# A linear-attention and PReLU feed-forward kernel: q of batch 0 loaded whole and first, w_out read in runs of four rows, w_in's columns taken with a step of four

## The chip, the cores and the metric

The kernel runs on one core of one Trainium2 chip. The metric is the time of one execution on the device in microseconds (us). The kernel before has a median of 294.09 us over 13 runs, which lie between 293.6 and 296.61 us.

## What is computed

The inputs are float32: q, k and v of shape (8, 8, 576, 64), g_norm (64), w_in (512, 2048), w_out (2048, 512) and alpha (2048). The output is (4608, 512) in float32.

```
kv  = einsum('bhsd,bhse->bhde', k, v)
o   = einsum('bhsd,bhde->bhse', q, kv)
o   = o / sqrt(mean(o*o, -1) + 1e-6) * g_norm
x   = o.transpose(0, 2, 1, 3).reshape(4608, 512)
h   = x @ w_in
g   = max(h, 0) + alpha * min(h, 0)
out = g @ w_out
```

The order of the 2048 columns of h is free: any permutation that is applied to the columns of w_in, to alpha and to the rows of w_out alike leaves the output as it is. The change uses this.

## The kernel before

**Tiling.** There are nine windows (`w`) of 512 tokens and 16 groups (`g`) of 128 columns of the hidden width. For a window, `m1_mm` makes one group of h with four matmuls of 128x512 (line 478), `m1_evac` turns it into fp16 `gt` with one ScalarE and one VectorE instruction (lines 485 and 487), and `y_mm` multiplies by a block of w_out (line 505). In window w the groups of h of that window alternate with four `y_mm` matmuls of window w-1.

**Attention.** k and q come into staging tiles `kst` and `qst` with 64 columns of a head beside each other, and `regroup` (line 112) copies them into `ksb` and `qsb`, where a pair of heads is one run of 128. `step_kv` (line 245) makes the k-v products of pairs of heads, `step_ot` and `half_ot` multiply by q, `ssq_mm` and `half_ssq` sum the squares and take the reciprocal root on ScalarE (Ln, then Exp), and `norm` writes `xt`, the input of the first product. Batches 0 and 1 transpose q on TensorE (`step_t`, line 221). From batch 2 on, q is transposed by DMA (line 383), and tiles go through four steps `tile_a` to `tile_d`: the product, the sum of squares on VectorE (line 409), the factor `rg` on GpSimd (line 421), and the product `xrow` on VectorE (line 430), which a DMA transpose (line 435) puts into `xm`.

**Order.** The order on every engine is written out by hand, and engines run their instructions in that order. `keep_warm(n)` issues n matmuls of 128x512 that nobody reads, to fill waits of TensorE at the start. `phase_steps(w + 1)` spreads the attention work of window w+1 over the groups of window w: `lags` says how many groups lie between `tile_a`, `tile_b` and `tile_c` (second entry), and `tile_d` (third entry). During window 1, `ys` are four PSUM banks with partial sums of window 0, and h uses the pools `H_POOL[0]`, `H_POOL[2]`, `S_POOL`, `H_POOL[1]` in turn.

**Loads.** All loads of q, k, v and of the weights are issued by GpSimd and turn float32 into fp16. Their order is: for each half of the heads of batch 0 its q, k and v (12 DMAs, since each piece is split into a long part, line 97, and a short part, line 102), then the four blocks of w_in, k of batch 1, the first block of w_out, q and v of batch 1, the other three blocks of w_out (line 173), then q, k and v of batch 2. Eight semaphores serve these DMAs in turn, so a DMA is issued once the eighth before it has landed.

A block of w_in has 512 neighbouring columns, and group r of it takes 128 neighbouring ones. A block of w_out has 512 rows, and partition p holds rows p, 128 + p, 256 + p and 384 + p, each a run of 2,048 bytes.

Of the kernel before, what the change touches and what calls it, by code (L numbers as in the profile page):

```python
# [17 lines left out]
def kernel(  # L18
# [27 lines left out]
    NC = D_MODEL // P  # L46
    assert NC == NPAIR and 0 < REM < P
    inv_d = 1.0 / D
    NB_PE = 2

    const_p = ctx.enter_context(tc.tile_pool(name="constp", bufs=1))
# [59 lines left out]
    def regroup(b, nm, h0=0, h1=H, eng=None):  # L111
        (eng or nc.vector).tensor_copy(  # L112
            out=bufs[b % NBUF][nm][:, :, h0:h1, :].rearrange("p t h d -> p h t d"),
            in_=stages[b % NBUF][nm][:, h0:h1],
        )
# [12 lines left out]
    ident = const_p.tile([P, P], FP32, name="ident")  # L128
    make_identity(nc, ident[:])
    HH = H // 2  # L130
    for h0 in (0, HH):
        for nm in "qkv":
            load(0, nm, h0, h0 + HH)

    mask32 = const_p.tile([P, P], FP32, name="mask32")
# [14 lines left out]
    g2col = const_p.tile([P, 1], FP32, name="g2col")  # L150
    nc.sync.dma_start(out=g2col[0:64, :], in_=g_norm[:].unsqueeze(1))
    nc.sync.dma_start(out=g2col[64:128, :], in_=g_norm[:].unsqueeze(1))
    alpha_row = const_p.tile([NF, P], FP32, name="alpha_row")
    nc.sync.dma_start(out=alpha_row[:], in_=moe_alpha[:].rearrange("(g p) -> g p", p=P))


    WQ = 4
    w_in_sb = []
    w_out_sb = []
    FW = D_FF // WQ  # L160
    GW = NF // WQ

    def load_w_in(i):
        t = w_p.tile([P, NC, FW], FP16, name=f"w_in_sb{i}")
# [6 lines left out]
    def load_w_out(i):  # L171
        t = w_p.tile([P, GW, D_MODEL], FP16, name=f"w_out_sb{i}")
        nc.gpsimd.dma_start(
            out=t[:],
            in_=moe_w_out[i * GW * P : (i + 1) * GW * P, :].rearrange("(g p) m -> p g m", p=P),
        )
        w_out_sb.append(t)

    def w_in_blk(c, g):
        i, r = divmod(g, GW)  # L180
        return w_in_sb[i][:, c, r * P : (r + 1) * P]

    def w_out_blk(g):
        i, r = divmod(g, GW)
# [50 lines left out]
    def step_kv(b, j0=0, j1=NPAIR, pool=(ps_s, "s")):  # L235
        if j0 == 0:
            kv_sb = attn_p.tile([P, NPAIR, P], FP16, name="kv_sb")
            for j in range(NPAIR):
                kvs[b, j] = kv_sb[:, j, :]
            kvs[b] = kv_sb  # L240
        kv_ps = pool[0].tile([P, j1 - j0, P], FP32, name="kv_ps", tag=pool[1])
        for j in range(j0, j1):
            ks, vs = pair_cols(b, "k", j), pair_cols(b, "v", j)
            for t in range(NT):
                nc.tensor.matmul(  # L245
                    out=kv_ps[:, j - j0, :], lhsT=ks(t), rhs=vs(t),
                    start=(t == 0), stop=(t == NT - 1),
                )
        nc.vector.tensor_mul(
            out=kvs[b][:, j0:j1, :], in0=kv_ps[:],  # L250
            in1=mask32[:].unsqueeze(1).to_broadcast([P, j1 - j0, P]),
        )
# [136 lines left out]
    def next_o():  # L389
        n_tile[0] += 1  # L390
        return ps_o, f"o{(n_tile[0] - 1) % 3}"
# [48 lines left out]
    def phase_steps(w):  # L440


        if w >= NW:
            return []
        todo = [(b, t) for b in range(NB_PE, min(B, w + 1)) for t in range(NT)
                if (b, t) not in done and b * S + t * P < (w + 1) * W]
        done.update(todo)
        steps = []

        kv_at = {NB_PE: 3, NB_PE + 1: 6, NB_PE + 2: 2}.get(w, 0)  # L450
        n = {NB_PE: 4, NB_PE + 1: 2}.get(w, 0)
        steps += [([], [], []) for i in range(n)]

        lags = (0, 1, 4) if w == NB_PE else (0, 1, 2)
        if w in (NB_PE + 1, NB_PE + 2):
            k = [b for b, t in todo].index(w)
            todo[k:k] = [None] * (3 if w == NB_PE + 1 else 1)
        for i in range(len(todo) + lags[2]):
            a, b, d = (
                [todo[i - k]] if 0 <= i - k < len(todo) and todo[i - k] else [] for k in lags  # L460
            )
            begin = [lambda x=x: tile_b(*x) for x in b] + [lambda x=x: tile_d(*x) for x in d]
            mid = [lambda x=x: tile_c(*x) for x in b]
            end = [lambda x=x: tile_a(*x) for x in a]
            steps.append((begin, mid, end))
        if w < B:
            steps[kv_at][1].append(lambda: step_kv(w, pool=next_o() if kv_at else (ps_s, "s")))
        return steps

    done = set()  # L470
# [10 lines left out]
            )  # L481

    def m1_evac(h_ps, w, g):
        m_sb = gt_p.tile([P, W], FP32, name="m_sb", bufs=3)
        nc.scalar.activation(out=m_sb[:], in_=h_ps[:], func=AF.Relu, scale=-1.0)  # L485
        gt = gt_p.tile([P, W], FP16, name="gt", tag=f"gt{g}")
        nc.vector.scalar_tensor_tensor(  # L487
            out=gt[:], in0=m_sb[:], scalar=beta_sb[:, g : g + 1], in1=h_ps[:],
            op0=ALU.mult, op1=ALU.add,
        )  # L490
        gts[w, g] = gt
# [38 lines left out]
    def spread_g():  # L530
# [13 lines left out]
    )  # L544
    step_t(0, 0, H_POOL[0])
    step_t(0, 1, H_POOL[1], nc.scalar)
    regroup(0, "k", 0, HH)
    load_rest()
    keep_warm(8)
    step_kv(0, 0, 2)  # L550
    keep_warm(2)
    step_ot(0, 0)
    step_ot(0, 1)
    keep_warm(1)
    regroup(0, "q", HH, H)
    ssq_mm(0, 0)
    step_t(0, 2, H_POOL[2])
    step_t(0, 3, H_POOL[0])
    alpha_ps = ps_h.tile([P, NF], FP32, name="alpha_ps", tag="h1")
    nc.tensor.matmul(  # L560
        out=alpha_ps[:], lhsT=alpha_row[:], rhs=ident[0:NF, 0:NF], is_transpose=True,
        start=True, stop=True,
    )

    beta_sb = const_p.tile([P, NF], FP32, name="beta_sb")
    nc.vector.tensor_scalar(
        out=beta_sb[:], in0=alpha_ps[:], scalar1=-1.0, scalar2=1.0, op0=ALU.mult, op1=ALU.add,
    )
    ssq_mm(0, 1)
    regroup(0, "k", HH, H)  # L570
    spread_g()
    norm(0, 0)
    keep_warm(2)
    step_kv(0, 2, 4)
    keep_warm(2)
    load_batch(2)
    half_ot(0, (ps_s, "s"))
    norm(0, 1)
    half_ot(1, (ps_y, "y"), nc.vector)
    first = [ps_h.tile([P, W], FP32, name="h_ps", tag=f"h{g}") for g in range(3)]  # L580
    first += [ps_o.tile([P, W], FP32, name="h_ps", tag=f"o{g}") for g in range(2)]
    half_ssq(0, O2)
    for g in range(4):
        m1_mm(first[g], 0, g, (0,))
    for g in range(4):
        if g == 2:
            half_ssq(1, O2)
        m1_mm(first[g], 0, g, (1,))
    for i in range(2):
        for c in (2, 3):  # L590
            for g in range(4):
                m1_mm(first[g], 0, g, (c,), slice(i * HW, (i + 1) * HW))
                if (i, c) == (1, 3):
                    m1_evac(first[g], 0, g)
        if i == 0:
            m1_mm(first[4], 0, 4, (0, 1))
# [66 lines left out]
    for w in range(1, NW):  # L663
        steps = phase_steps(w + 1)
        for g in range(NF):
            if g == LOAD_G and 4 < w + 2 < B:
                load_batch(w + 2)
            a, part = divmod(g, TPW)
            parts = range(part * TPW, (part + 1) * TPW)
            if w == 1:  # L670
                a, y = TPW - 1, ys[TPW - 1]
                parts = [LATER + g] if LATER + g < NF else []
            begin, mid, end = steps.pop(0) if steps else ([], [], [])
            for f in begin:
                f()
            m1_group(w, g, [H_POOL[0], H_POOL[2], S_POOL, H_POOL[1]][g % 4] if w == 1 else None)
            for f in mid:
                f()
            if 0 in parts:
                pool, tag = ((ps_y, "y"), (ps_s, "s"))[a % 2]  # L680
                y = pool.tile([P, W], FP32, name="y_ps", tag=tag)
            for gg in parts:
                y_mm(y, w - 1, a, gg)
            if NF - 1 in parts:
                y_out(y, w - 1, a)
            for f in end:
                f()
            if (w, g) == (1, 0):
                regroup(2, "k", eng=nc.gpsimd)
            if (w, g) == (1, 2):  # L690


                gate = const_p.tile([1, 1], FP16, name="gate")
                nc.gpsimd.tensor_copy(out=gate[:], in_=qtms[2][0:1, 0, 0:1])
                load(3, "q")
                load(3, "k")
            if (w, g) == (1, 8):
                regroup(3, "q", eng=nc.gpsimd)
            if (w, g) == (1, 11):

                nc.gpsimd.tensor_copy(out=gate[:], in_=xm(2)[0:1, 0, W - 1 : W])
                load(3, "v")
                transpose_q(3)
                regroup(3, "k", eng=nc.gpsimd)
            for i in {5: (0, 1), 6: (2, 3), 7: (4,), 8: (5,)}.get(g, ()) if w == 2 else ():
                load_part(4, "qkv"[i // 2], i % 2 == 0)
            if w > 1 and g == LOAD_G + 3 + 3 * (w == 2) and w + 2 < B:
                regroup_batch(w + 2)
            if w > 1 and g == NF - 3 and w + 2 < B:
                transpose_q(w + 2)  # L710
# [43 lines left out]
```

## Time and profile before

| What | Value |
|---|---|
| Median of 13 runs | 294.09 us |
| The profiled execution, its own time | 294.84 us |
| Its span in the profile | 292.7 us |
| Granted TensorE clock | 0.998 |
| TensorE busy | 281.5 us (96% of the span) |
| Weight loads busy | 138.2 us (47%) |
| VectorE, ScalarE, GpSimd busy | 169.2, 152.8, 100.1 us |
| Bytes read from HBM | 36.71 MB |

The span is the time from the first to the last instruction of the program; the execution's own time is 2.14 us longer. Busy shares are averages over the whole span, so they do not say which engine a stage waits for. For that one reads the idle time ahead of an instruction and what ended it, and the chain of work that ended last.

### The profile page before, as it was taken

What the parts mean: (1) busy time and instruction counts of PE and PEld (TensorE: products, weight loads), DVE (VectorE), ACT (ScalarE), POOL (GpSimd) and SP (SyncE); (2) the same over time, 40 slices, a digit from 0 to 9 for tenths busy, and PEclk for the clock granted to TensorE, in tenths of its full rate; (3) what the DMA queues carried; (4) which work ended last, traced back from release to release, by engine and by line L of the source; (5) the groups of instructions that cost most, each with busy time, mean ns of one, the idle gap of its engine ahead of it and who ended that gap; (6) DMA issues with size and microseconds to landing.
All of it is one profiled execution on the core that took longest, in us unless ns stands there. A gap on an engine that the chain in (4) does not pass through costs nothing.

```text
span 292.7 us, 4287 instructions
## 1 busy us (share of the span) xinstructions
PE 281.5 (96%) x1551; PEld 138.2 (47%) x1551; DVE 169.2 (58%) x261; ACT 152.8 (52%) x297; POOL 100.1 (34%) x111
## 2 busy tenths in 40 slices
PE   5999889999999999999999999999999999999994
PEld 2554444543454454455445544554445444444443
DVE  4579846787668476447844874488447644444300
ACT  1459357585646466447644754466448544444211
POOL 8832420584448227333743383324003200000000
PEclk9999999999999999999999999999999999999999
DMA  6999999999999925991599269925212311122133
GB/s 82 186 206 203 200 207 196 186 184 176 137 146 190 180 35 84 199 213 36 93 196 219 52 106 181 199 55 83 54 36 56 81 36 38 45 47 48 43 72 72
DMA packets 66228, 35.54 MB, mean 121 GB/s; under 512 B 32784, under 2 KB 61728, under 8 KB 66208
## 3 DMA queue, kind: packets, MB, share of 16 engines
q0 software_dynamic: 29664, 18.35, 45.6%
q1 hardware_dynamic: 36384, 16.80, 29.0%
q8 instruction: 12, 0.20, 0.3%
q10 hardware_dynamic: 160, 0.13, 0.2%
q14 instruction: 8, 0.07, 0.1%
HBM read 36.71 MB, written 9.44 MB: 158 GB/s over the span
## 4 chain that ended last, share of the span: by engine, by line
PE 76%; DMA 17%; DVE 2%; POOL 2%; ACT 1%; issue 1%; POOLq 0%; DVEq 0%
PE y_ps L505 38%; PE h_ps L478 33%; DMA vst<-in_v_dram 5%; DMA w_in_sb<-in_moe_w_in_dram 5%; DMA w_out_sb<-in_moe_w_out_dram 5%; PE kv_ps L245 2%; PE otm_ps L397 2%; DMA kst<-in_k_dram 2%; DVE gt L487 1%; DMA xm<-xrow 1%; POOL w_in_sb L165 1%; DVE ss L409 1%; DVE xrow L430 1%; ACT sqm_sb L403 0%; POOL qst L97 0%
## 5 line engine op out<-in xcount | busy, mean ns | idle before, releaser
L487 DVE SCALAR_TENSOR_TENSOR gt<-m_sb,beta_sb,h_ps 128x512 f16<-128x512 f32 x144 | 105.7, 744 | 75.4 <-ACT m_sb L485 74.9
L485 ACT ACTIVATE m_sb<-h_ps 128x512 f32<-128x512 f32 x144 | 85.5, 597 | 87.6 <-PE h_ps L478 86.3
L505 PE MATMUL y_ps<-w_out_sb,gt 128*128 128x512 f16 (+1 forms) x528 | 128.8, 373 | 0.0
L478 PE MATMUL h_ps<-xm,w_in_sb 128*128 128x512 f16 x448 | 115.0, 379 | 0.7 <-DMA xm<-xrow 0.7
L505 PEld LDWEIGHTS <-gt 128*128 128x128 f16 x592 | 57.6, 98 | 64.5
L478 PEld LDWEIGHTS <-w_in_sb 128*128 128x128 f16 x584 | 55.8, 98 | 62.2 <-issue 2.4
L421 POOL TENSOR_TENSOR rg<-ss,g_all 128x512 f32<-128x512 f32 (+1 forms) x30 | 31.3, 1042 | 78.1 <-ACT ss L419 69.8
L478 PE MATMUL h_ps<-xt,w_in_sb 128*128 128x512 f16 (+1 forms) x136 | 30.4, 366 | 0.2 <-ACT y_sb L515 0.2
L515 ACT COPY y_sb<-y_ps 128x512 f32<-128x512 f32 (+1 forms) x32 | 18.4, 575 | 15.9 <-PE y_ps L505 15.9
L409 DVE TENSOR_REDUCE ss<-sqm_sb 128x8 f32<-128x512 f32 (+1 forms) x30 | 20.5, 683 | 10.5 <-ACT sqm_sb L403 10.5
L430 DVE TENSOR_TENSOR xrow<-otm_ps,rg 128x512 f16<-128x512 f32 (+1 forms) x30 | 20.5, 682 | 3.6 <-POOL rg L421 3.6
L403 ACT ACTIVATE sqm_sb<-otm_ps 128x512 f32<-128x512 f32 (+1 forms) x30 | 17.7, 590 | 6.3 <-PE otm_ps L397 6.3
L112 POOL COPY ksb<-kst 128x2560 f16<-128x2560 f16 x6 | 13.9, 2324 | 14.8 <-DMA kst<-in_k_dram 14.8
L112 POOL COPY qsb<-qst 128x2560 f16<-128x2560 f16 x5 | 11.6, 2317 | 10.8 <-issue 10.8
L397 PEld LDWEIGHTS <-qtm 128*128 128x128 f16 x120 | 9.2, 98 | 7.1
L204 PE MATMUL warm_ps<-warm,mask 128*128 128x512 f16 x25 | 8.5, 478 | 3.3 <-DVE eps_t L146 3.3
L397 PE MATMUL otm_ps<-kv_sb,qtm 128*128 128x128 f16 x120 | 11.6, 219 | 0.0
L245 PE MATMUL kv_ps<-vst,ksb 128*128 128x128 f16 x160 | 10.4, 219 | 0.9 <-DMA vst<-in_v_dram 0.7
L245 PEld LDWEIGHTS <-ksb 128*128 128x128 f16 x160 | 9.4, 98 | 3.8 <-issue 1.7
L416 ACT ACTIVATE ss<-ss,eps_t 128x8 f32<-128x8 f32 (+1 forms) x30 | 9.0, 301 | 3.2 <-DVE ss L409 2.9
L513 DVE COPY y_sb<-y_ps 128x256 f32<-128x256 f32 x1 | 0.4, 423 | 13.4 <-PE y_ps L505 13.4
L102 POOL DMA_DIRECT2D vst<-in_v_dram x9 | 6.3, 697 | 4.3 <-DMA w_in_sb<-in_moe_w_in_dram 2.0
(76 smaller groups left out, 136.1 us busy)
## 6 DMA issues: line engine op xcount, KB each, us to landing
out_dram<-y_sb SPq DMA_DIRECT2D x70, 128.0 KB, 2.3
kst<-in_k_dram POOLq DMA_DIRECT2D x7, 320.0 KB, 8.4
qst<-in_q_dram POOLq DMA_DIRECT2D x7, 320.0 KB, 5.1
vst<-in_v_dram POOLq DMA_DIRECT2D x7, 320.0 KB, 10.7
w_in_sb<-in_moe_w_in_dram POOLq DMA_DIRECT2D x4, 512.0 KB, 10.2
w_out_sb<-in_moe_w_out_dram POOLq DMA_DIRECT2D x4, 512.0 KB, 15.2
kst<-in_k_dram POOLq DMA_DIRECT2D x7, 256.0 KB, 9.4
qst<-in_q_dram POOLq DMA_DIRECT2D x7, 256.0 KB, 6.7
```

The source lines that it names most:

```text
L112: (eng or nc.vector).tensor_copy(out=bufs[b % NBUF][nm][:, :, h0:h1, :].rearrange("p t h d -> p h t d"), in_=stages[b % NBUF][nm][:, h0:h1],)
L245: nc.tensor.matmul(out=kv_ps[:, j - j0, :], lhsT=ks(t), rhs=vs(t), start=(t == 0), stop=(t == NT - 1),)
L397: nc.tensor.matmul(out=ot_ps[:, 2 * j : 2 * j + 2, :], lhsT=qtms[b][:, t * NPAIR + j, :], rhs=kvs[b, j], start=True, stop=True,)
L403: nc.scalar.activation(out=sq[0:n], in_=ot_ps[0:n], func=AF.Square)
L409: nc.vector.tensor_reduce(out=ss[0:n], in_=sq[0:n], op=ALU.add, axis=mybir.AxisListType.X,)
L421: nc.gpsimd.tensor_tensor(out=rg[0:n], in0=ss[0:n].unsqueeze(2).to_broadcast([n, H, D]), in1=g_all[0:n].unsqueeze(1).to_broadcast([n, H, D ...
L430: nc.vector.tensor_mul(out=x[0:n], in0=ot_ps[0:n], in1=rg[0:n])
L478: nc.tensor.matmul(out=h_ps[:, cols], lhsT=w_in_blk(c, g), rhs=xt_of(w, c)[:, cols], start=(c == 0), stop=(c == NC - 1 and cols.stop == W),)
L485: nc.scalar.activation(out=m_sb[:], in_=h_ps[:], func=AF.Relu, scale=-1.0)
L487: nc.vector.scalar_tensor_tensor(out=gt[:], in0=m_sb[:], scalar=beta_sb[:, g : g + 1], in1=h_ps[:], op0=ALU.mult, op1=ALU.add,)
L505: nc.tensor.matmul(out=y[:], lhsT=gts[w, g][:, a * P : (a + 1) * P], rhs=w_out_blk(g)[:, cols], start=(g == 0), stop=(g == NF - 1),)
L515: nc.scalar.copy(out=y_sb[:, cols], in_=y[:])
```

## The change

- **q of batch 0** is loaded with all eight heads in two DMAs ahead of everything else, in place of two DMAs for each half. k and v of batch 0 are still loaded in halves, behind it. Batch 0 takes 10 DMAs in place of 12.
- **w_out** is read with partition p holding rows 4p to 4p+3 of a block, which are one run of 8,192 bytes. Column r of such a four stands in group r, so `w_in_blk` takes every fourth column of its block: 128 fp16 elements with a step of 8 bytes. alpha is read as 4 rows of 512, transposed with four small matmuls in place of one, and `m1_evac` looks its column up as `u`.
- **The order at the start**: all four transposes of q, the transposes of alpha and `spread_g` now stand ahead of the first `step_kv`. The second `step_t` copies of a pair, the squares of `step_ot(0, 1)` and those of `half_ot(1)` change engines; `half_ssq(0)` and `half_ot(1)` move between the first matmuls of h, and `half_ssq(1)` behind the second four. The sum of the `keep_warm` matmuls stays 25.
- **Window 1**: the third lag for window 2 goes from 4 to 3, `step_kv` of batch 2 moves behind the `y_mm` of its group, and the h pools of groups 1 and 2 (of every four) change places.

```diff
     HH = H // 2
+    load(0, "q")
     for h0 in (0, HH):
-        for nm in "qkv":
+        for nm in "kv":
             load(0, nm, h0, h0 + HH)
...
-    alpha_row = const_p.tile([NF, P], FP32, name="alpha_row")
-    nc.sync.dma_start(out=alpha_row[:], in_=moe_alpha[:].rearrange("(g p) -> g p", p=P))
+    alpha_row = const_p.tile([WQ, FW], FP32, name="alpha_row")
+    nc.sync.dma_start(out=alpha_row[:], in_=moe_alpha[:].rearrange("(i f) -> i f", f=FW))
...
-            in_=moe_w_out[i * GW * P : (i + 1) * GW * P, :].rearrange("(g p) m -> p g m", p=P),
+            in_=moe_w_out[i * GW * P : (i + 1) * GW * P, :].rearrange("(p r) m -> p r m", p=P),
...
-        return w_in_sb[i][:, c, r * P : (r + 1) * P]
+        return w_in_sb[i][:, c, r:FW:GW]
...
-        lags = (0, 1, 4) if w == NB_PE else (0, 1, 2)
+        lags = (0, 1, 3) if w == NB_PE else (0, 1, 2)
...
-            steps[kv_at][1].append(lambda: step_kv(w, pool=next_o() if kv_at else (ps_s, "s")))
+            steps[kv_at][2 if w == NB_PE else 1].append(lambda: step_kv(w, pool=next_o() if kv_at else (ps_s, "s")))
...
+        u = g % GW * WQ + g // GW
...
-            out=gt[:], in0=m_sb[:], scalar=beta_sb[:, g : g + 1], in1=h_ps[:],
+            out=gt[:], in0=m_sb[:], scalar=beta_sb[:, u : u + 1], in1=h_ps[:],
...
     step_t(0, 1, H_POOL[1], nc.scalar)
-    regroup(0, "k", 0, HH)
-    load_rest()
-    keep_warm(8)
-    step_kv(0, 0, 2)
-    keep_warm(2)
-    step_ot(0, 0)
-    step_ot(0, 1)
-    keep_warm(1)
     regroup(0, "q", HH, H)
-    ssq_mm(0, 0)
     step_t(0, 2, H_POOL[2])
-    step_t(0, 3, H_POOL[0])
+    step_t(0, 3, H_POOL[0], nc.scalar)
     alpha_ps = ps_h.tile([P, NF], FP32, name="alpha_ps", tag="h1")
-    nc.tensor.matmul(
-        out=alpha_ps[:], lhsT=alpha_row[:], rhs=ident[0:NF, 0:NF], is_transpose=True,
-        start=True, stop=True,
-    )
+    for r in range(GW):
+        nc.tensor.matmul(
+            out=alpha_ps[:, r * WQ : (r + 1) * WQ], lhsT=alpha_row[:, r:FW:GW],
+            rhs=ident[0:WQ, 0:WQ], is_transpose=True, start=True, stop=True,
+        )
...
+    spread_g()
+    regroup(0, "k", 0, HH)
+    load_rest()
+    keep_warm(7)
+    step_kv(0, 0, 2)
+    keep_warm(2)
+    step_ot(0, 0)
+    step_ot(0, 1, eng=nc.vector)
+    regroup(0, "k", HH, H)
+    keep_warm(2)
+    ssq_mm(0, 0)
+    keep_warm(2)
     ssq_mm(0, 1)
-    regroup(0, "k", HH, H)
-    spread_g()
+    step_kv(0, 2, 4)
     norm(0, 0)
-    keep_warm(2)
-    step_kv(0, 2, 4)
     keep_warm(2)
     load_batch(2)
     half_ot(0, (ps_s, "s"))
     norm(0, 1)
-    half_ot(1, (ps_y, "y"), nc.vector)
...
-    half_ssq(0, O2)
     for g in range(4):
         m1_mm(first[g], 0, g, (0,))
+        if g == 1:
+            half_ssq(0, O2)
+            half_ot(1, (ps_y, "y"))
     for g in range(4):
-        if g == 2:
-            half_ssq(1, O2)
         m1_mm(first[g], 0, g, (1,))
+    half_ssq(1, O2)
...
-            m1_group(w, g, [H_POOL[0], H_POOL[2], S_POOL, H_POOL[1]][g % 4] if w == 1 else None)
+            m1_group(w, g, [H_POOL[0], S_POOL, H_POOL[2], H_POOL[1]][g % 4] if w == 1 else None)
```

More of the change, by code (lines that the diff above doesn't have):

```diff
@@ L48 @@
     inv_d = 1.0 / D
+    WQ = 4
+    FW = D_FF // WQ
+    GW = NF // WQ
     NB_PE = 2
@@ L152 @@
     nc.sync.dma_start(out=g2col[64:128, :], in_=g_norm[:].unsqueeze(1))
-    alpha_row = const_p.tile([NF, P], FP32, name="alpha_row")
-    nc.sync.dma_start(out=alpha_row[:], in_=moe_alpha[:].rearrange("(g p) -> g p", p=P))
-    WQ = 4
+    alpha_row = const_p.tile([WQ, FW], FP32, name="alpha_row")
+    nc.sync.dma_start(out=alpha_row[:], in_=moe_alpha[:].rearrange("(i f) -> i f", f=FW))
     w_in_sb = []
     w_out_sb = []
-    FW = D_FF // WQ
-    GW = NF // WQ
     def load_w_in(i):
```

## The prediction

> **What bounds the kernel now.** I read the page's slices first, then the chain of waits in order of time, then TensorE's timeline around each wait, then the busy time by stage. The page:
>
> ```profile
> PE   5999889999999999999999999999999999999994
> DMA  6999999999999925991599269925212311122133
> ```
>
> TensorE is full but for the ends, and the DMA engines are full for the first 14 slices of 7.3 us. The chain of waits, in order of time (start, us, what):
>
> ```profile
> 3.43 5.47 DMA kst<-in_k_dram
> ...
> 12.22 13.97 DMA w_in_sb<-in_moe_w_in_dram
> 26.48 13.73 DMA w_out_sb<-in_moe_w_out_dram
> 40.49 14.04 DMA vst<-in_v_dram
> 54.66 1.28 PE kv_ps L245 x20
> ...
> 66.86 2.62 DMA xm<-xrow
> 69.62 1.02 PE h_ps L478 x4
> ```
>
> Up to 54.5 us the end is set by loads, up to 69.6 us by the chain from batch 2 to xm, and then by matmuls alone. Busy time by stage (stretch, its length, busy us and instructions of PE, PEld, DVE, ACT, POOL; clock; DMA share; GB/s):
>
> ```profile
> 38.00:42.60 4.60, 4.27 (x38) 2.47 (x36) 2.08 (x3) 2.07 (x4) 1.35 (x2) 1.00 1.24 207
> 45.00:51.00 6.00, 6.00 (x31) 2.71 (x30) 4.05 (x7) 4.55 (x8) 0.00 (x0) 1.00 1.40 198
> 72.00:102.00 30.00, 30.00 (x173) 14.97 (x172) 18.63 (x28) 17.10 (x36) 16.39 (x15) 1.00 1.09 164
> ```
>
> The first stretch loads w_out, the second q and k; the third shows TensorE without a gap. TensorE's timeline (start, us, what, idle before it):
>
> ```profile
> 35.62 1.29 PE L221 MATMUL qt_ps<-ident,qsb 128*128 128x128 f16 x20 [0.83 <-DVE qsb L112]
> 37.82 1.28 PE L245 MATMUL kv_ps<-vst,ksb 128*128 128x128 f16 x20 [0.47 <-DMA vst<-in_v_dram]
> 39.88 0.36 PE L278 MATMUL ot_ps<-qt_sb,kv_sb 128*128 128x448 f16 x1 [0.33 <-DVE kv_sb L249]
> 51.23 1.02 PE L478 MATMUL h_ps<-xt,w_in_sb 128*128 128x512 f16 x4 [0.18 <-ACT y_sb L515]
> 54.66 1.28 PE L245 MATMUL kv_ps<-vst,ksb 128*128 128x128 f16 x20 [0.25 <-DMA vst<-in_v_dram]
> ...
> 69.62 1.02 PE L478 MATMUL h_ps<-xm,w_in_sb 128*128 128x512 f16 x4 [0.67 <-DMA xm<-xrow]
> ```
>
> A matmul of 512 columns shows 0.38 us, but the next starts 0.216 us after it (four in 0.86 us). Counted from the starts before them, the gaps are 0.99, 0.63, 0.49, 0.34, 0.41 and 0.86 us. After 69.62 us nothing is left to gain without less TensorE work, and the change removes none there.
>
> **Head.** The landings of batch 0 in the trace are: q's first half 5.59 us, k's 8.90, v's 10.36, q's second half 11.93, k's 13.37, v's 14.94, the first block of w_in 17.46. Two issues fewer (about 0.6 us each on GpSimd) save nothing: the DMA engines have a backlog, and the same bytes precede w_in. All later loads move up by two places, and each still waits for the eighth before it. Whole q lands 1.57 us after its first half if its second 288 KB go as fast as now (10.36 to 11.93), at 7.2 us; at 8.90 if they take the 3.31 us that k's first half takes now. I take 7.2, since it is the row of the same tensor. k's and v's first halves then land one place later, at 10.36 and 11.93.
>
> TensorE's order after that: regroup (0.55 us) from 7.3, ten transposes, a copy and the second regroup (0.46 + 0.55), ten transposes, to about 10.2; four alpha transposes at about 0.2 (one float32 transpose and its load show 0.14 to 0.23) to 11.0; `spread_g` 0.35; seven fillers 1.51, to 12.85. v allows the first `step_kv` from 12.07. So it starts at 12.1 to 12.85 in place of 10.50; I take 12.4, half way.
>
> What follows, in offsets from that start, by durations and spacings of the present rows: the masked product is read by `step_ot` at 1.24; VectorE's copy and square of `ot(0,1)`, 0.69 each, end at 3.26; the second k regroup ends at 3.74 and `step_kv(0,2,4)` starts at 3.83; `half_ot(0)` at 5.07. ScalarE has its two Ln/Exp pairs until 5.4, then the square of half 0 (5.50), Ln (6.56), Exp (7.28), the square of half 1, now ScalarE's (7.81), its ssq matmul (8.46), Ln (8.87), Exp (9.59), the xt product (10.25), and the last half of c = 2 on TensorE at 10.79. From 12.07 that is 22.86 us, from 12.85 it is 23.64, and now it is 21.24: the head is 1.6 to 2.4 us later; I take 2.0. The squares of half 1 have left VectorE and stand before Ln of half 1 on ScalarE, with the first `m1_evac` queued behind.
>
> **Where that delay goes.** TensorE arrives at q of batch 1 0.99 us early today and at its v 0.63 us early; with the 0.34 us at 51.23 (h now takes `S_POOL`, free since 50.05, in place of the bank that ScalarE's copy of y holds), 1.96 us of waits can be eaten. Without them it would reach `step_kv` of batch 2 not at 54.25 (54.66 less its 0.41) but at 54.25 - 1.96 = 52.3 us, and the `y_mm` now ahead of it makes 52.5. With the delay of 2.0 it is 54.5.
>
> **Loads.** v of batch 2 allows 54.66 us. Four blocks of w_out precede it. Runs that write 512 to 640 bytes move 198 GB/s, runs of 1,024 bytes 207. With a fixed cost per run on top of a rate, runs of 4,096 written bytes come to 216 GB/s: 524,288 bytes take 2.42 us in place of 2.53, 0.11 us a block, 0.4 us in all, 0.1 of it before q of batch 1. No row shows a run of 8 KB, so I keep -0.4 to +0.4 us, and take +0.4, the direction of the two rows. v then allows 54.26, TensorE comes at 54.5, and it has one matmul (0.22 us) more behind it than now: gain 54.66 + 0.22 - 54.5 = 0.4 us.
>
> **The xm chain.** VectorE is back to back from 61.90 us: sum, gt, xrow, gt, xrow, gt, xrow, the last at 65.67. With the third lag at 3 the gt ahead of the first xrow falls behind the last, so it starts at 65.02: 0.65 us earlier. Its factor is ready at 64.28 (GpSimd 63.24 + 1.04). The SyncE transpose at 66.86, queued behind two others, moves as much. The wait of 0.86 us shrinks to 0.2. What is late next is TensorE itself. The gt that now waits costs nothing while h has four banks; without that cover it is 0.65 us.
>
> **Strided weight loads.** There are 584 loads of w_in now (busy us and mean ns behind the first bar):
>
> ```profile
> L478 PEld LDWEIGHTS <-w_in_sb 128*128 128x128 f16 x584 | 55.8, 98 | 62.2 <-issue 2.4
> ```
>
> A load may take until the matmul before it is done, 0.216 us; 98 ns leaves 118. No row of before steps over elements. The nearest, a float32 load of alpha, shows 135 ns for twice the bytes. I take no cost; at the other end, four times the row (392 ns) is 176 ns too long, 101 us for 576.
>
> [...]
>
> **Sum.** 0.4 + 0.65 = 1.05 us off the profiled execution's 294.84 us gives 293.8. That execution is 0.75 us above the median, so the median goes to 293.0. What a measurement can tell from no change is 0.3%, 0.9 us.
>
> **Rivals.**
> *The head outruns its cover (slower).* If whole q lands at 8.90, the order above puts the first `step_kv` at 14.55 and the last half of c = 2 at 25.34: 4.1 us late. TensorE then reaches `step_kv` of batch 2 at 56.6, 1.7 us later than now with its extra matmul; less the xm gain that is 1.1 us slower, 295.2. It decides from a delay of 3.05 us (52.5 + 3.05 = 54.88 + 0.65). For it: DMA moves 149 GB/s from 5 to 9 us and 187 from 9 to 13.5, and I don't know whether that belongs to k or to the time. Against it: q's own rows. Chance 0.2, with 0.02 of it too small to tell.
> *No difference to be told.* The head is 2.4 us late, kv gains nothing, and 0.65 us of xm are left: 293.4. Chance 0.19, with 0.02 over the bound.
> *Strided loads over 0.216 us.* Every 10 ns above it cost 5.8 us. Against it: 118 ns of room. Chance 0.06.
> *More is gained.* The head is only 1.0 us late, w_out brings over 1 us, and xm's wait goes whole: 54.88 - 53.5 + 0.86 = 2.2 us, 291.9. Chance 0.06.
>
> **How the numbers follow.** The forecast has 0.49, and its own range is 292.4 to 293.7 (gains of 1.6 to 0.4 us); 0.44 of it is over the bound. Faster: 0.44 + 0.06 + 0.02 = 0.52. Slower: 0.18 + 0.06 = 0.24. Same: 0.05 + 0.17 + 0.02 = 0.24. The range goes from 291.9 to 295.2, the ends of the second last and the first rival; beyond are the strided loads and the edges of those two.
>
> **What would show it.** In the profile after: q regrouped near 7.3 us; `step_kv` of batch 0 near 12.4; no wait for q or v of batch 1 on TensorE; `step_kv` of batch 2 near 54.5; the first matmul on xm with at most 0.2 us of wait; weight loads of w_in below 216 ns with TensorE at 30.00 of 30 us in the middle. A first matmul on xm past 69.6 us or gaps in the middle would make the prediction wrong.

## The result, and the profile after

The changed kernel takes 296.63 us in the median of 11 runs (295.01 to 297.98), beside 294.07 us for the kernel before in 48 runs. The ratio is 1.0085 with a 95% interval of 1.0066 to 1.0103: it is slower by 2.6 us. The prediction was 293.0 us in a range of 291.9 to 295.2. In one kernel further down (k of batch 3 loaded later, with window 1) two executions, 302.08 and 298.11 us at clocks of 0.987 and 0.991, lie more than 1.5% above its fastest and are left out of its ratio and median; no trace of them was kept.

The profiled execution of it took 294.63 us, with a span of 292.5 us and a granted clock of 0.999. That is 0.2 us less than the profiled span before, and 2.0 us less than the median of the same kernel, so the page alone does not show the loss. It does show what moved. The slices of the page (tenths of busy time in 40 slices of 7.3 us):

```profile
PE   5889999999999999999999999999999999999994
DMA  7999999997999915991599279934212311122133
```

TensorE is below nine tenths in the first 22 us only (before, in the first 44 us), and the DMA engines show seven tenths in the tenth slice (66 to 73 us), where they were full before. The chain of work that ended last, in order of time (start, us, what):

```profile
2.27 5.20 DMA qst<-in_q_dram
...
23.48 10.98 PE h_ps L481 x54
37.39 1.29 PE qt_ps L224 x20
39.11 1.13 PE kv_ps L248 x20
...
66.79 3.61 PE h_ps L481 x16
```

Before, loads held the end up to 54.5 us. Now they hold it only until q of batch 0 has landed (2.27 + 5.20 = 7.47 us). From there it is the first chain of attention, and from 23.5 us on it is TensorE. Busy time by stage, in the same stretches as before (length; PE, PEld, DVE, ACT, POOL; clock; DMA share; GB/s):

```profile
38.00:42.60 4.60, 4.28 (x48) 2.87 (x45) 2.20 (x5) 2.28 (x4) 0.68 (x1) 1.00 1.09 208
45.00:51.00 6.00, 6.00 (x34) 2.82 (x32) 4.18 (x6) 4.20 (x7) 0.93 (x1) 1.00 1.39 199
72.00:102.00 30.00, 30.00 (x173) 15.86 (x172) 18.55 (x27) 17.36 (x36) 15.24 (x14) 1.00 1.12 165
```

In the last stretch TensorE is still busy for 30.00 of 30 us. TensorE's timeline after (start, us, what, idle before it), first the head and then the places where it waited before:

```profile
8.12 0.83 PE L224 MATMUL qt_ps<-ident,qsb 128*128 128x128 f16 x10 [0.43 <-DVE qsb L117]
9.63 0.73 PE L224 MATMUL qt_ps<-ident,qsb 128*128 128x128 f16 x10 [0.68 <-DVE qsb L117]
...
11.23 1.69 PE L207 MATMUL warm_ps<-warm,mask 128*128 128x512 f16 x7
12.75 0.72 PE L248 MATMUL kv_ps<-vst,ksb 128*128 128x128 f16 x10
...
23.48 3.84 PE L481 MATMUL h_ps<-xt,w_in_sb 128*128 128x256 f16 x21 [0.66 <-DVE xt L339]
...
37.39 1.29 PE L224 MATMUL qt_ps<-ident,qsb 128*128 128x128 f16 x20 [0.35 <-DVE qsb L117]
38.95 1.28 PE L248 MATMUL kv_ps<-vst,ksb 128*128 128x128 f16 x20
41.01 0.80 PE L281 MATMUL ot_ps<-qt_sb,kv_sb 128*128 128x448 f16 x5 [0.32 <-DVE kv_sb L252]
50.94 1.03 PE L481 MATMUL h_ps<-xt,w_in_sb 128*128 128x512 f16 x4
55.25 1.28 PE L248 MATMUL kv_ps<-vst,ksb 128*128 128x128 f16 x20
69.38 1.03 PE L481 MATMUL h_ps<-xm,w_in_sb 128*128 128x512 f16 x4
```

The waits for v of batch 1, for the bank at 51 us, for v of batch 2 and for xm are gone. A wait ahead of q of batch 1 is left, and one that had not been there stands before a matmul at 66.79 us. Counted from start to start, as the prediction counts them, the two executions differ by these terms:

| Place | Before, us | After, us | Difference |
|---|---|---|---|
| start of the last half of c = 2 | 21.24 | 23.48 | +2.24 |
| wait ahead of q of batch 1 | 0.99 | 0.52 | -0.47 |
| wait ahead of v of batch 1 | 0.64 | 0 | -0.64 |
| wait at 51 us for a bank | 0.35 | 0 | -0.35 |
| wait ahead of `step_kv` of batch 2 | 0.41 | 0 | -0.41 |
| wait for xm | 0.84 | 0 | -0.84 |
| wait for an h bank at 66.8 us | 0 | 0.25 | +0.25 |
| sum | | | -0.22 |

The sum is the difference of the two spans, 292.5 - 292.7, and from the first matmul on xm to the end it is 223.1 us in both (292.7 - 69.62 and 292.5 - 69.38). So the profiled pair is explained, and what is to be found is why the other executions of the changed kernel are slower than the profiled one. Their list of spans and clocks gives the first hint: 292.9 us at 1.0, 294.0 to 295.0 us at 0.994, 295.5 and 295.8 us at 0.988 and 0.986 (and one of 295.7 us with a clock given as 1.0). The first theory was therefore that the new head leaves TensorE too sparsely used to keep its clock; the rivals were the strided weight loads, the new order itself, and the changes in window 1.

### The profile page after: what moved, and what is told of

It is laid out like the page before. It is cut to its first block, busy times and chain, and to the rows that moved or that the text cites. A ratio compares the mean times of both kernels' runs of the same rounds, so it can differ in the third digit from the quotient of the medians.

```text
span 292.5 us, 4293 instructions
## 1 busy us (share of the span) xinstructions
PE 281.4 (96%) x1554; PEld 147.0 (50%) x1554; DVE 168.3 (58%) x260; ACT 153.6 (53%) x298; POOL 98.2 (34%) x109
## 4 chain that ended last, share of the span: by engine, by line
PE 89%; DVE 4%; ACT 2%; DMA 2%; issue 1%; POOL 1%; DVEq 0%; POOLq 0%
PE h_ps L481 39%; PE y_ps L509 38%; PE kv_ps L248 3%; PE otm_ps L400 2%; DMA qst<-in_q_dram 2%; DVE gt L491 1%; PE ya L509 1%; PE yb L509 1%; PE yc L509 1%; PE qt_ps L224 1%; PE warm_ps L207 1%; DVE xrow L433 1%; DVE qsb L117 1%; PE ssq_ps L297 1%; PE ot_ps L281 1%
## 5 line engine op out<-in xcount | busy, mean ns | idle before, releaser
L481 PEld LDWEIGHTS <-w_in_sb 128*128 128x128 f16 x584 | 64.4, 113 | 54.9 <-issue 2.5
L234 ACT COPY qt_sb<-qt_ps 128x576 f16<-128x576 f16 x4 | 2.5, 638 | 10.8 <-PE qt_ps L224 10.8
```

The lines of the kernel that those rows point to most:

```text
L481: nc.tensor.matmul(out=h_ps[:, cols], lhsT=w_in_blk(c, g), rhs=xt_of(w, c)[:, cols], start=(c == 0), stop=(c == NC - 1 and cols.stop == W),)
```

## The experiments

There are three groups of four kernels. The first four (up to the fillers that hold up the clock) and the next four (window 1 alone, with the permutation, q of batch 0 whole, fillers moved) ran on one chip, the last four (all but the order, too few fillers, k of batch 3 later in two kernels) on another. Each group has its own runs of the kernel before, with medians of 294.17, 293.99 and 293.98 us, and ratios are to these. Each kernel has one profiled execution.

### The changed kernel again

No edit.

> The changed kernel unaltered. Its profiled execution had a span of 292.5 us at a granted clock of 0.999, while most of its other executions show 294.0 to 295.8 us at 0.986 to 0.994. Clock theory: a stretch of about 3.4 us at half clock costs about 1.7 us, and TensorE's waits for q at 7.5 to 9.6 us bring such stretches on in most executions; so the median stays near 296.5 us, spans near 292.5 go with a clock of 0.998 or more and longer ones with 0.994 or less, with 1.5 to 2 us for each 0.006 of clock. Rival (strided weight loads): time lost in the middle of the kernel at full clock, so long executions at 0.999 with gaps between matmuls after 72 us.

Measured: 297.93 us, ratio 1.0125 [1.0103, 1.0146]. This time the profiled execution is one with a low clock (span 296.0, clock 0.988), and its timeline can be laid beside the one above:

```profile
8.79 0.73 PE L224 MATMUL qt_ps<-ident,qsb 128*128 128x128 f16 x10 [1.62 <-DVE qsb L117]
10.31 1.25 PE L224 MATMUL qt_ps<-ident,qsb 128*128 128x128 f16 x10 [0.79 <-DVE qsb L117]
...
12.68 3.17 PE L207 MATMUL warm_ps<-warm,mask 128*128 128x512 f16 x7
15.64 1.26 PE L248 MATMUL kv_ps<-vst,ksb 128*128 128x128 f16 x10
...
26.90 0.27 PE L481 MATMUL h_ps<-xt,w_in_sb 128*128 128x256 f16 x1 [0.65 <-DVE xt L339]
```

Ten transposes take 0.73 us at 8.79 and 1.25 us at 10.31; seven fillers take 3.17 us where the profiled execution above has 1.69. The busy time by stretch of the same execution (columns as above, the clock third from the right):

```profile
6.51:9.92 3.41, 1.39 (x13) 0.66 (x11) 1.43 (x4) 0.36 (x1) 2.10 (x4) 1.00 1.40 195
9.92:13.34 3.42, 3.03 (x18) 2.32 (x19) 1.52 (x5) 0.91 (x2) 3.40 (x6) 0.50 1.39 196
13.34:16.75 3.41, 3.41 (x17) 1.87 (x16) 0.88 (x4) 0.00 (x0) 1.59 (x3) 0.50 1.25 206
```

TensorE was busy for 1.39 of 3.41 us while it waited for q and its regroup, and the two following stretches of 3.41 us ran at half clock. `step_kv` starts 2.89 us later than in the other execution (15.64 against 12.75), of which 0.67 is q, which landed at 8.14 instead of 7.47 us; the last half of c = 2 starts 3.42 us later, and the span is 3.5 us longer. Nothing behind 27 us gives any of it back.

### The permutation alone, and the change without it

```diff
 # the first: in the kernel before
-        return w_in_sb[i][:, c, r * P : (r + 1) * P]
+        return w_in_sb[i][:, c, r:FW:GW]
 ... w_out as p * 4 + r, alpha and its column u as in the change
 # the second: in the changed kernel, the same lines turned back
```

> The kernel before with only the permuted hidden width: w_out in runs of four rows, w_in's columns with a step of four, alpha's four transposes. Loads and order of the start and of window 1 as before. Clock theory (the head is to blame): clock 0.998, weight loads of w_in about 113 ns as in the changed kernel, time like the kernel before or up to 0.5 us less, 293.6 to 294.2 us. Rival (strided weight loads lower the clock or the matmul rate): 296 us or more at a clock of 0.994 or less.

> The changed kernel with the hidden width not permuted: w_in, w_out and alpha are read as before, the new loads and order of the start and window 1 stay. Clock theory (the head is to blame): median 296 to 297 us, clock mostly 0.994 or less. Rival (strided weight loads): 294 us or less at a clock of 0.998.

Measured: the permutation alone takes 293.9 us, ratio 0.9985 [0.9971, 0.9999]; the change without it takes 296.14 us, ratio 1.0056 [1.0033, 1.0079]. The loads of the weights of w_in, first in the changed kernel, then in the change without the permutation (busy us and mean ns behind the first bar):

```profile
L481 PEld LDWEIGHTS <-w_in_sb 128*128 128x128 f16 x584 | 64.4, 113 | 54.9 <-issue 2.5
L481 PEld LDWEIGHTS <-w_in_sb 128*128 128x128 f16 x584 | 55.8, 98 | 61.5 <-issue 2.6
```

A strided load takes 113 ns in place of 98, well below the 216 ns from one matmul to the next, and TensorE is busy for 30.00 of 30 us from 72 to 102 us in the profile above. So the loss does not come from the permutation. The executions without the permutation also show the clock by itself, since nothing else differs between them: three have spans of 292.1 to 292.5 us at 0.997 to 0.999, eight have 293.8 to 294.4 us at 0.992 to 0.994, one has 296.0 us at 0.988. By an estimate from the 3.41 us at half clock in the trace above, each 0.006 of clock is one such stretch (0.5 x 3.41 / 293 = 0.0058); between the first two groups it costs some 1.8 us.

### The clock held up by fillers

```diff
-    keep_warm(10)
+    keep_warm(12)
...
     regroup(0, "q", HH, H)
+    keep_warm(4)
     step_t(0, 2, H_POOL[2])
```

> The changed kernel with six more filler matmuls that nobody reads: 12 in place of 10 at the start, and 4 between the second and the third transpose step of q, where TensorE waits 0.64 and 0.84 us. Clock theory: TensorE is busy from 3.3 to 9.6 us, the clock goes back to 0.998 and the median to 293.5 to 294.5 us, 2 us or more less than the changed kernel. Rival (strided weight loads): no gain, 296 to 297 us, and up to 0.3 us more for the fillers.

Measured: 295.5 us, ratio 1.0044 [1.003, 1.0058]. Six more matmuls that nobody reads make the kernel 2.4 us faster than the same kernel without them on the same chip (297.93), and all 11 executions lie between 295.22 and 295.64 us with clocks of 0.997 to 1.0. The fillers only add work, so at least these 2.4 of the 3.8 us that the changed kernel loses on this chip are the clock's. But 1.3 us over the kernel before are left at full clock, where up to 0.5 us was expected; the new order was the open suspect.

### Window 1 alone, and with the permutation

```diff
-        lags = (0, 1, 4) if w == NB_PE else (0, 1, 2)
+        lags = (0, 1, 3) if w == NB_PE else (0, 1, 2)
 ... step_kv of batch 2 at [2], S_POOL and H_POOL[2] exchanged, as in the change
```

> The kernel before with only the three edits of window 1: third lag 3, step_kv of batch 2 behind the y matmul, h pools of two groups exchanged. By the prediction's terms: step_kv of batch 2 still waits for v (one matmul of 0.22 us more behind it), the wait of 0.34 us for ScalarE's copy goes, xm's wait of 0.86 us falls to 0.2: 0.6 to 0.9 us less, 293.2 to 293.6 us, clock 0.998. Rival (the gt that now waits holds an h bank, as a wait of 0.26 us in the changed kernel hints): 0.3 us less or nothing, 293.8 to 294.2 us.

> The kernel before with the permuted hidden width and the three edits of window 1; loads and order of the start stay. If the two parts add up: 293.0 to 293.4 us at a clock of 0.998 or more, faster than both kernels. If the head is what the changed kernel loses by, this is 2.5 us or more below it. Rival (window 1 or the strided loads bring the loss): 295 us or more.

Measured: 294.18 us, ratio 1.0001 [0.9985, 1.0017], and with the permutation 293.68 us, ratio 0.9991 [0.9976, 1.0007], above the 293.0 to 293.4 us that the two parts would give if they added up. So the 0.65 us that the third lag was to bring do not come. TensorE's timeline of window 1 alone shows the wait for xm not shorter but longer (1.04 us idle against 0.67; both profiled executions lie above the median of their kernel):

```profile
69.87 1.02 PE L478 MATMUL h_ps<-xm,w_in_sb 128*128 128x512 f16 x4 [1.04 <-DMA xm<-xrow]
```

The chain of waits of that stretch gives the last transpose (start, us):

```profile
66.11 3.62 DMA xm<-xrow
```

The third transpose is issued at 66.11 us, 0.75 us earlier than before (66.86), and lands at 66.11 + 3.62 = 69.73 us, 0.25 us later than before (69.48). In both executions the three transposes land one after the other right behind the last piece of k of batch 3 (it lands at 67.93 us before and at 68.30 us here; the transposes at 68.52, 69.06, 69.48 and at 68.76, 69.30, 69.73). The loads of batch 3 had been issued earlier, and in these two executions the transposes land only after them. The `gt` that now stands behind the last `xrow` also makes TensorE wait 0.25 us for a bank of h at 66.08 us.

### q of batch 0 whole, nothing else

```diff
+    load(0, "q")
     for h0 in (0, HH):
-        for nm in "qkv":
+        for nm in "kv":
```

> The kernel before with only the load of q changed: whole and first, k and v in halves behind it. The order on the engines stays, fillers too. TensorE then waits for q from 7.5 us to 8.2 to 8.8 us. Clock theory: the wait is enough to bring stretches of half clock in a part of the executions, median 295 to 297 us and a wide spread (over 1.5 us from lowest to highest); those at full clock lie near 294 us. Rival (only the new order of the engines is to blame): 293.8 to 294.3 us, spread as before, clock 0.998.

Measured: 293.68 us, ratio 0.9992 [0.9976, 1.0009]. In TensorE's timeline the first transposes wait for q like those of the changed kernel:

```profile
8.45 0.73 PE L222 MATMUL qt_ps<-ident,qsb 128*128 128x128 f16 x10 [1.36 <-DVE qsb L112]
9.01 1.89 PE L205 MATMUL warm_ps<-warm,mask 128*128 128x512 f16 x8
```

The wait is followed at once by eight fillers, so in its stretch from 6.35 to 9.76 us TensorE is busy for 2.05 of 3.41 us and keeps the full clock; all 12 executions have clocks of 0.997 to 1.0. One gap of 1.4 us alone did not lose it here, so the 295 to 297 us of the clock theory were wrong for this kernel. What the changed order adds are a second wait and, behind it, only small matmuls before the fillers.

### Fillers moved, and the whole change but its order

```diff
 # fillers moved: the kernel with six more fillers, and
-    keep_warm(7)
+    keep_warm(2)
     step_kv(0, 0, 2)
 # all but the order: whole q, the permutation and window 1 of the change,
 # with the calls between step_t(0, 1) and the second four m1_mm in the order of the kernel before
```

> The kernel with six more fillers (12 at the start, 4 between the transposes), with 2 in place of 7 fillers ahead of the first step_kv. With 7, step_kv of batch 0 starts at 13.4 us although its v has landed at 11.1. If the fillers set that start, it comes at 12.3 to 12.5 us, all of the head moves up by about 1 us, and the median falls from 295.5 to 294.4 to 294.8 us at a clock of 1.0. Rival (late q sets it): 295.3 us or more. If the clock is lost again for want of fillers, the spread exceeds 1 us and the median is 296 us or more.

> The changed kernel with the old order of the engines at the start: whole q first, permuted hidden width and the three edits of window 1, but transposes, alpha, fillers, squares and half steps as in the kernel before. If the new order is the whole loss, this is 293.2 to 293.9 us, below the kernel before by up to 0.3%, with full clock after the start. If whole q and the permuted width only lose together, 295 us or more. The wait for xm should stay at 0.5 to 1.1 us in spite of the third lag of 3, since the transposes land only after k of batch 3.

Measured: 294.78 us, ratio 1.0025 [1.0014, 1.0036], and 293.48 us, ratio 0.9988 [0.9971, 1.0004]. All executions of both have clocks of 0.997 to 1.0, and q lands alike in the two profiles (8.05 and 8.13 us). TensorE's timelines, first with fillers moved and the new order, then with the old order:

```profile
8.70 0.73 PE L224 MATMUL qt_ps<-ident,qsb 128*128 128x128 f16 x10 [0.17 <-DVE qsb L117]
...
10.27 0.73 PE L224 MATMUL qt_ps<-ident,qsb 128*128 128x128 f16 x10
10.93 0.64 PE L557 MATMUL alpha_ps<-ident,alpha_row 4*128 4x4 f32 x4
...
12.65 0.73 PE L248 MATMUL kv_ps<-vst,ksb 128*128 128x128 f16 x10 [0.18 <-DVE ksb L117]
```

```profile
8.78 0.73 PE L222 MATMUL qt_ps<-ident,qsb 128*128 128x128 f16 x10 [1.11 <-DVE qsb L115]
9.35 1.89 PE L205 MATMUL warm_ps<-warm,mask 128*128 128x512 f16 x8
11.28 0.72 PE L246 MATMUL kv_ps<-vst,ksb 128*128 128x128 f16 x10
```

The second pair of transposes and the alpha and g matmuls ahead of `step_kv` put it 1.37 us later; the wait of 0.18 us is for VectorE's regroup of k, which stands behind the copies of these results. From there to the last half of c = 2 it is 10.88 us in the new order (23.53) and 11.04 us in the old one (22.32, both from the chain of waits), so only 0.16 us of it comes back. The difference at c = 2, 1.21 us, is close to the difference of the medians, 1.30 us. The two kernels ran on different chips and differ in their fillers too, but their ratios to the kernel before lie apart.

The expectation had a wait of 0.5 to 1.1 us for xm in the kernel with all but the order. It is 0.13 us in this profile: the transposes again land behind k of batch 3 (66.71 us; 67.80 and 68.22), but TensorE comes there later, after a wait of 0.25 us for a bank of h.

### Too few fillers in the kernel before

```diff
-    keep_warm(10)
+    keep_warm(4)
...
     load_rest()
-    keep_warm(8)
     step_kv(0, 0, 2)
```

> The kernel before with 4 in place of 10 fillers at the start and none in place of 8 ahead of the first step_kv; nothing else. No load and no result that is used comes later by this: the first transposes can even start at 6.3 us in place of 7.5. Clock theory: TensorE is then idle from 5.0 to 6.3 and from 7.4 to 10.4 us, the full clock comes 3.4 us or 6.8 us later or is taken back, and the median rises by 1.5 to 3.5 us to 295.5 to 297.5 us, with the half clock seen in the profile between 8 and 17 us. Rival (the clock has no part, only late data): 294.0 us, as before.

Measured: 294.93 us, ratio 1.0021 [1.0005, 1.0036], that is 0.95 us slower by the medians (0.6 by the ratio), less than was expected. Its TensorE's timeline shows all transposes up to 15 us at the duration of the low clock (1.25 to 1.27 us for ten, 0.73 at full clock):

```profile
6.30 1.25 PE L221 MATMUL qt_ps<-ident,qsb 128*128 128x128 f16 x10 [1.18 <-DVE qsb L112]
10.39 1.23 PE L245 MATMUL kv_ps<-vst,ksb 128*128 128x128 f16 x10 [2.84 <-DVE qst L91]
...
13.97 1.27 PE L221 MATMUL qt_ps<-ident,qsb 128*128 128x128 f16 x10
```

And the busy time by stretch (columns as above; the record has no grant before 15.36 us, and the column of the clock shows 1.00 there):

```profile
5.12:8.54 3.42, 1.25 (x11) 0.99 (x10) 1.37 (x3) 0.64 (x1) 3.26 (x6) 1.00 1.22 154
8.54:11.95 3.41, 1.56 (x12) 1.20 (x12) 1.60 (x5) 0.00 (x0) 2.67 (x4) 1.00 1.35 186
11.95:15.36 3.41, 3.41 (x17) 1.85 (x15) 1.06 (x4) 2.20 (x4) 3.32 (x6) 1.00 1.30 192
```

Here the full clock comes 7 us later than before (15.36 us in place of 8.34), with the old order, the old loads and no later data: `step_kv` still starts at 10.39 us, but the last half of c = 2 starts at 22.68 us in place of 21.24. By the medians, the waits for loads behind it took up about a third of these 1.44 us. So too few fillers cost time by the clock alone; the price depends on the waits that follow. (The mean clock of this execution is given as 0.998, although the record has no full clock before 15.36 us: the mean counts from the first grant on. So the execution of the changed kernel with 295.7 us at "1.0" may be one with a late first grant, which no run shows.)

### k of batch 3 loaded later

```diff
             if (w, g) == (1, 2):
...
                 load(3, "q")
-                load(3, "k")
             if (w, g) == (1, 8):
                 regroup(3, "q", eng=nc.gpsimd)
+                load(3, "k")
```

> The kernel with the permuted hidden width and the three edits of window 1, and besides the load of k of batch 3 is issued behind GpSimd's regroup of q of batch 3, some 8 us later. In the kernel without this the first matmul on xm waits 1.12 us, and xm's transposes land only 0.5 us after k of batch 3 although they are issued earlier. If those loads hold the transposes back, the wait falls to 0.3 us or less and the median by 0.7 to 1.1 us, to 292.6 to 293.0 us. Rival (the transposes themselves are slow, or k is then late for batch 3): 293.7 us or more, and a new wait of TensorE at step_kv of batch 3 near 80 us.

> Whole q first, permuted hidden width, window 1's three edits, k of batch 3 later, and the old order at the start. If the parts add up, the least of all: 292.3 to 293.0 us, 0.4 to 0.6% below the kernel before. If TensorE is then bound by its own work up to 69 us, no less than the kernel without whole q first.

Measured: 294.36 us in the median of ten executions, ratio 1.0014 [0.9996, 1.0032], with the permutation and window 1; 293.18 us, ratio 0.9989 [0.9967, 1.0011], with all of the change but the order. TensorE's timeline of the first:

```profile
67.90 1.03 PE L478 MATMUL h_ps<-xm,w_in_sb 128*128 128x512 f16 x4
...
80.86 1.28 PE L245 MATMUL kv_ps<-vst,ksb 128*128 128x128 f16 x20 [1.12 <-DMA vst<-in_v_dram]
```

With k out of the way the transposes issued at 64.03 and 65.34 us land at 66.47 and 67.77 us, and xm is no longer waited for. This agrees with k's load having held them. But then v of batch 3 is late, and a wait is back 13 us further on, 1.3 us from start to start. The second kernel has 0.58 us left at xm and 1.43 us at `step_kv` of batch 3. The wait moved: the first is no faster than the kernel before, and the second cannot be told from the one with all but the order and early k. The profiled execution of the second, 295.17 us, is one of five at 294.5 to 295.6 us; the other seven lie at 292.9 to 293.2 us, and whether they have these waits no trace shows.

## Why the prediction was wrong

**The head's delay was right, its clock was not thought of.** The prediction had q at 7.2 us, `step_kv` at 12.4 and the last half of c = 2 2.0 us late; the profiled execution has 7.47, 12.75 and 2.24. The start of `step_kv` lies near the upper end of its range, 12.85, which the order sets; the lower end went by v of the first half landing at 11.93 us, and it landed at 10.44. But the step "seven fillers 1.51, to 12.85" takes the spacing of the full clock for granted. That spacing was the old head's: there TensorE was without a gap from 3.25 to 10.34 us, as its timeline before shows:

```profile
3.25 4.42 PE L204 MATMUL warm_ps<-warm,mask 128*128 128x512 f16 x10 [3.25 <-DVE eps_t L146]
7.47 1.14 PE L221 MATMUL qt_ps<-ident,qsb 128*128 128x128 f16 x10
8.45 1.89 PE L204 MATMUL warm_ps<-warm,mask 128*128 128x512 f16 x8
10.50 0.72 PE L245 MATMUL kv_ps<-vst,ksb 128*128 128x128 f16 x10 [0.16 <-DVE qst L91]
```

The new one waits twice for the regroup of q and then runs small matmuls, and by the estimate from the mean clocks of its executions (0.994 and 0.986 to 0.988) the clock falls for one or two stretches in most of them. No rival had this in it. Between the profiled execution (294.63 us) and the median (296.63 us) it is 2.0 us, the largest part of the loss; it is shown by the fillers that bring 2.4 us back, and by the kernel before, which loses 0.6 to 0.95 us with fewer of them. The miss of 3.6 us is these 2.0, the 0.8 by which the profiled execution missed its own forecast (294.63 against 293.8), and the 0.75 that was taken off for the median.

**The cover was too large.** "1.96 us of waits can be eaten" counted 0.99 us at q of batch 1 whole. The line shown there says that VectorE ended it. About 0.52 us of it is VectorE's own sequence ahead of `regroup`, which moves with the head: it stands at 0.52 us in the changed kernel and in nearly all the experiments. In this pair of profiles the cover is 1.44 us. With it the prediction's own sum gives 54.25 - 1.44 + 2.24 + 0.22 = 55.27 us for `step_kv` of batch 2, and the profile has 55.25, against 54.5 predicted.

**An execution is not the median.** The sum was made for an execution 0.75 us above the median, whose loads were late, and 0.75 was then taken off. In the profiled execution of the permutation alone (293.52 us, with the old head) TensorE waits 0.25 us for v of batch 1 and not at all for v of batch 2. There the cover is smaller still. So at full clock the changed kernel is not 0.2 us faster, as in the pair of profiles, but slower: the 294.63 and 295.01 us of its two best executions are 0.6 and 0.9 us over the median before, and the kernels with fillers 0.8 and 1.3 us.

How far every microsecond of the head counts is seen over four kernels with whole q and the permutation (start of the last half of c = 2 in the profile; median of all executions):

| Kernel | c = 2, us | Time, us |
|---|---|---|
| all but the order | 22.32 | 293.48 |
| fillers moved | 23.53 | 294.78 |
| six more fillers | 24.10 | 295.5 |
| the changed kernel again | 26.90 | 297.93 |

Between the first two rows 1.21 us of delay stand beside 1.30 us of time, between the second and the last 3.37 beside 3.15: past 22.3 us the delay is paid almost in full. The kernel with the permutation and window 1 but the old loads and order stands at 21.26 us and 293.68 us; against it the first 1.1 us of delay cost nothing.

**The xm term had the wrong cause.** That the transpose "moves as much" was wrong with the old head: the issue moved, the landing did not, and it came right behind k of batch 3. The "gt that now waits costs nothing while h has four banks" was wrong too, by 0.25 us. In the changed kernel the wait for xm does go: k of batch 3 lands at 66.50 us, before the third transpose is issued (66.68), this one lands 2.44 us later at 69.12, and TensorE is late. What the lag does there is not shown, since no kernel has the new head with the old lag.

**What was right.** The strided loads cost nothing (113 ns each, with TensorE busy for 30.00 of 30 us). The last blocks of w_out come 2.50 and 2.45 us apart in the kernel with the permutation alone, against 2.51 and 2.58 before and 2.42 predicted; over all profiles the second and the third are 2.39 to 2.84 us apart with the permutation and 2.51 to 2.59 without, so the predicted 0.11 us a block is not clear. The waits for v of batch 1 and 2 went. The rival that outruns its cover named the right side, with the wrong condition: q did not land at 8.90 us but at 7.4 to 8.1, and its deciding delay of 3.05 us becomes 2.53 us when the cover is 0.52 us smaller. The profiled execution, with a delay of 2.24 us at full clock, stands just short of that point; one half-clock stretch, at the 1.8 us estimated above, takes it past.

No version beats the kernel before by what can be told with ease: the permutation alone has the only interval below 1 (0.9971 to 0.9999), and all but the order reaches 1.0004.

**What the prediction had at nothing.** That two issues fewer "save nothing" is not what the profiles have: with whole q first, the first block of w_in lands at 15.98 to 16.74 us in eight of them, with the old loads at 16.56 to 17.46 us in six. Why, no run shows.

## What to carry to other kernels

When a change moves the head of a kernel, look at how densely TensorE is used there in each stretch of a few microseconds, not only at when each step is ready: fillers that were spread through the waits belong with the waits, and a pair of waits (1.62 and 0.79 us) with small matmuls between and behind them cost a clock that one wait of 1.36 us, with fillers behind it, did not. Before a wait is counted as cover, read what ends it: what ends with a load is cover, what ends with an engine's own sequence moves along. And lay the profiled execution beside the list of all executions with their spans and clocks, since one profile can be the best of its kernel.

## What the hardware showed

In the execution of the changed kernel with the low clock TensorE has the full clock from 6.51 us, half of it from 9.92 to 16.75 us, and the full clock again behind that: steps after 3.41 and 6.83 us. They lie at different times in each execution: in the other profile of the same kernel the first full clock begins at 8.36 us. After a stretch with TensorE busy for 1.39 of 3.41 us (41%) the clock was gone; after 2.05 (60%, q of batch 0 whole), 2.30 (all but the order) and 2.73 of 3.41 (the changed kernel's first profile) it stayed:

```profile
6.35:9.76 3.41, 2.05 (x18) 1.06 (x16) 1.61 (x4) 0.55 (x1) 2.55 (x5) 1.00 1.40 195
8.36:11.77 3.41, 2.73 (x29) 2.13 (x27) 1.94 (x6) 1.28 (x2) 3.23 (x6) 1.00 1.39 196
```

A loss of the clock at the start is in one trace only, and the longest gap ahead of it was 1.62 us, against 1.36 us where q of batch 0 is whole and the clock stayed. So whether the share of a stretch or the gap goes with the loss is open, and so is whether small matmuls count for less. What brings the full clock back is not settled: in the execution with the low clock half clock went on after a stretch with 3.03 of 3.42 us busy, and in the other the full clock came after one with 2.98 of 3.41 us.

A 16-bit weight load of w_in with elements 8 bytes apart takes 113 ns in the changed kernel, against 98 without the permutation. The next matmul starts 216 ns after the one before, so the 15 ns more are hidden: TensorE is busy for 30.00 of 30 us there.

With window 1 alone, DMA transposes that SyncE issued at 62.9 to 66.1 us landed only behind k of batch 3, which GpSimd had issued at 58.5 and 59.2 us. Issuing the last of them 0.75 us earlier than in the kernel before did not make it land earlier (69.73 us against 69.48).
